# Sliding-window attention and a gated MLP in one kernel: first batch rearranged, work taken off GpSimd, and a new planned order

## The chip, the cores and the metric

One core of a Trainium2 chip. The metric is the time of one execution on the device in microseconds (us), median of several runs. Engines: TensorE (PE; PEld is its weight load), VectorE (DVE), ScalarE (ACT), GpSimd (POOL) and SyncE (SP). DMAs are issued here by GpSimd (loads that also turn float32 into bfloat16) and by SyncE (stores, transposing DMAs).

## The reference

```
q, k, v: [8 batches, 8 heads, 576, 64]
scores = q k^T / 8
heads 0-3: keep 0 <= row - col < 32                            (plain)
heads 4-7: keep 0 <= row - col < 128, (row - col) % 4 == 0     (dilated)
x = softmax(masked scores) v, heads side by side               # [4608, 512]
h = x w_in                                                     # w_in [512, 2048]
g = h / (1 + exp(-beta h))                                     # beta [2048]
out = g w_out                                                  # w_out [2048, 512], float32
```

## The kernel before

The MLP (called the MoE part in the code) runs over 9 tiles of 512 tokens. For each tile, `slot_h` makes 16 blocks of 128 columns of h (line 901: four matmuls of 512 columns over the four parts of x, `xT`), a tanh on ScalarE (line 910) and the gate on VectorE (line 915, into `g`). `block` makes 4 blocks of 128 output rows (line 936: 16 matmuls each, in four parts of four), an eviction (line 951 or 953) and a store (line 956). x for a tile comes from `attention(b)`, which works out batch b, so batch 0 must be done before the first matmul of line 901, and the other batches are worked out between the matmuls of earlier tiles.

`attention` for batches 0 to 2 (`DIRECT = 3`) loads q and k to `st`, transposes them on TensorE (lines 483 and 493) and evicts them to `dk`, `dq`, `kT`, `qT`; later batches go by a bfloat16 copy in DRAM (`s`) and transposing DMAs. Names: S2, S3 are dilated scores (line 697), S00 to S11 plain scores (line 761; line 725 from batch 3 on), T the tail's; V and U are values (lines 802, 818, 787), each followed by a reciprocal and a multiplication on VectorE (lines 652, 653); X and Y carry x back by transposes (lines 855, 870, 840) and copies into `xT`, in batches 0 and 1; later batches use DMAs. In `exp_and_mask` the exp is on ScalarE (line 633). Batch 0 adds its masks on TensorE, with `add_d` and `add_p`, before the scores; later batches multiply by `mask_n` or `mask_d` afterwards (line 637), on GpSimd or VectorE. `spread` copies the values from where they landed (`vd16`) to `vd`, where each row of 64 has a 1 behind it, so that the value matmul also gives the sum. `halo` copies the last 32 rows of each block of `vp` to the next block. Copies all go through line 257, loads through line 408.

Nothing is issued in program order. Each step is a `plan.op` with the engines that could do it, their costs in ns, its dependences and a due time `vt`. `Plan.run` is a list scheduler: it takes the step that can start first, among nearly equal ones that with the earliest due time, and writes each engine's instructions in the order found. `NUDGE` shifts the start that it sees for single steps, `CAPS` says how many PSUM banks each kind of step may hold ("o" are output blocks), and `DVE` and `POOL` exclude each other for steps marked `sbuf`. Where TensorE would be idle for long, the planner puts in fillers, matmuls of zeros (line 1057: twelve small ones, for the first nine; line 1059: one of 256 columns). At run time only semaphores set the times, and each engine follows its written order.

The weights are loaded once: `w_in_bf` in three DMAs (512, 512 and 1024 columns), `w_out_bf` in two halves, all on GpSimd's queue among the loads of batches 0 and 1. The first four h blocks are split (`APART = 4`): first the dilated half of x, then the plain half in two pieces of tokens.

Of the kernel before, what the change touches and what calls it, by code (L numbers as in the profile page):

```python
# [10 lines left out]
ACT = mybir.ActivationFunctionType  # L11
# [3 lines left out]
COLD = 5500  # L15
# [25 lines left out]
class Plan:  # L41
# [4 lines left out]
    CAPS = {"h": 4, "p": 4, "o": 3, "z": 4, "a": 8, "s": 5, "w": 6}  # L46
    SWITCH = 95
    NUDGE = {6: 2500, 32: -2500, 44: 150, 45: -400, 58: -150, 72: 60, 76: -400, 88: -400, 96: 60,
# [10 lines left out]
    LAT = {"PE": 210, "ACT": 45, "DVE": 45, "POOL": 60, "SP": 0}  # L59
    NEAR = {"PE": 40, "ACT": 60, "DVE": 60, "POOL": 60, "SP": 0}  # L60
# [12 lines left out]
    def run(self, filler=None, filler_until=0.0):  # L73
# [14 lines left out]
        halves = False  # L88
        issued = 0.0
        port = {"DVE": 0.0, "POOL": 0.0}  # L90
# [20 lines left out]
        while n_left:  # L111
            best = None
            near = {}
            for o in avail:
# [3 lines left out]
                if o.sbuf and "POOL" in at:  # L118
                    at["POOL"] = max(at["POOL"], issued)
                if o.sbuf:  # L120
                    at = {e: max(t, port["DVE" if e == "POOL" else "POOL"]) for e, t in at.items()}
# [19 lines left out]
            if filler is not None and s <= filler_until and free["PE"] + (300 if free["PE"] < COLD else 170) < s:  # L141
# [5 lines left out]
                free["PE"] = now + (225 if now < COLD else 115)  # L147
# [12 lines left out]
            free[e] = s + d  # L160
            if o.sbuf:
                port[e] = s + d
            elif o.dma and e == "POOL":
                issued = s + d + 1200
# [34 lines left out]
def kernel(  # L199
# [39 lines left out]
    AT_ONCE = 3  # L239

# [91 lines left out]
    fill1 = plan.op([("DVE", 300)], t_fill1, vt=-8)  # L332
# [4 lines left out]
    fill2 = plan.op([("DVE", 1500)], t_fill2, vt=-7.9)  # L337
# [13 lines left out]
    fill4 = plan.op([("POOL", 800)], t_fill4, vt=-1.2)  # L351
# [35 lines left out]
    adds = {"D": plan.op([("POOL", 900)], t_add_d, vt=-8.96)}  # L387
    adds["P"] = plan.op([("POOL", 1250)], t_add_p, vt=-7.5)
    par = plan.op([("DVE", 600)], t_parity, [ident], vt=-7.9)
    mask_tail = plan.op([("POOL", 1150)], t_mask_t, [par], vt=-7.295)  # L390
# [30 lines left out]
    def first_keys():  # L421
# [5 lines left out]
        return [plan.op([("ACT", 175 + .834 * RD * D), ("DVE", 160 + 1.042 * RD * D)],  # L427
                        lambda e, x=x: copy(e, std[0][:, x], stage[:, x]), [o], -9.1, sbuf=True) for x in range(2)]

    def direct_vp(b, deps, vt):  # L430
# [3 lines left out]
        for hs in ((slice(0, 4),) if b else (slice(0, 2), slice(2, 4))):  # L434
# [7 lines left out]
            out.append(plan.op([("DVE", 160 + .27 * n * 320), ("POOL", 170 + 1.04 * n * 320)], halo, [o],  # L442
# [108 lines left out]
    def attention(b, ld, names, vts):  # L551
# [43 lines left out]
        o = plan.op([("DVE", 450), ("POOL", 550), ("ACT", 500)], mixed,  # L595
# [5 lines left out]
        for c in range(2):  # L601
# [4 lines left out]
            o = plan.op([("DVE", 250), ("POOL", 500), ("ACT", 290)], padded,  # L606
# [12 lines left out]
        def spread(e):  # L619
            copy(e, vd[kv][:, :, :, 0:D], vd16_of[b])  # L620
        o = plan.op([("POOL", 1100), ("DVE", 620), ("ACT", 1030)], spread,
                    [ld["vd"][0], (fill3, fill4)[kv]] + war(("vd", kv)), vt, sbuf=True)
        used("vd16" if b < DIRECT else ("st", kv), o)
        wrote(("vd", kv))
        vdeps["D"] = [o]
# [4 lines left out]
        def exp_and_mask(key, sop, g, vt, n, sc, w, m, tiles):  # L630
# [3 lines left out]
            ex = plan.op([act(n)], expo, [sop, fill2] + war(*tiles), vt - .005, group=g)  # L634
            if b >= ADDED or key == ("T",):
                def mask(e):
                    E[e].tensor_tensor(out=w(), in0=w(), in1=m(), op=ALU.mult)  # L637
                ex = plan.op([("POOL", 170 + 2.2 * n), ("DVE", 160 + .8 * n)], mask,
                             [ex] + [mask_tail if key == ("T",) else mask_ops["D" if key[0] in (2, 3) else "n"]],
                             vt, sbuf=True)  # L640
# [3 lines left out]
        def normed(key, vop, g, vt, n, blocks, pv, dst, war_key):  # L644
# [11 lines left out]
            vdone[key] = plan.op([("DVE", 310 + 1.042 * blocks * D)], norm, [vop] + war(war_key), vt - .003, group=g)  # L656

        for name in [n for n in names if n[0] in "ST"]:
# [54 lines left out]
            j = int(name[2])  # L713
            if b >= AT_ONCE:
# [56 lines left out]
            for n, x in enumerate(xs):  # L771
                for h in range(2):
# [5 lines left out]
                                 [("pt", x, i) for i in range(3 * j, 3 * j + 3)])  # L778
        for name in [n for n in names if n[0] in "VU"]:
# [17 lines left out]
            if x >= 2:  # L797
                def values(e, x=x, j=j, g=g):
                    pv = bank(g)[:, 0:4 * (D + 1)].rearrange("p (r h e) -> p r h e", r=2, h=2)
                    for r in range(2):  # L800
                        for a in range(2):
                            nc.tensor.matmul(pv[:, r, a], lhsT=ptd[:, x - 2, j, 2 * r + a],  # L802
                                             rhs=vd[kv][:, 2 * (x - 2) + a, 2 * r + j, 0:D + 1],
                                             start=True, stop=True)
                vop = plan.op([("PE", 4 * mm(D + 1))], values, [sdone[x, j]] + vdeps["D"], vt, acquire=g)
# [287 lines left out]
```

## Time and profile before

| what | us |
|---|---|
| median of 3 runs (299.75 to 299.88) | 299.83 |
| profiled execution: span from first to last instruction | 298.3 |
| the profiled execution's own time | not given apart from its span |
| TensorE busy | 293.0 (98%) |
| VectorE busy | 186.1 (62%) |
| ScalarE busy | 169.8 (57%) |
| GpSimd busy | 90.4 (30%) |
| first matmul of line 901 starts at | 18.44 |
| last store issued at | 295.59 |

The page shows busy times and the chain of waits that ended last. A window row gives the busy time of each engine in a stretch. A timeline row gives start, length, engine, line, operation, what is written and read, and the idle time in front with what ended it. A DMA row gives size and the median time from issue to landing. A group row gives busy time and mean ns of one instruction, then the idle time in front. Matmuls are pipelined, so that the lengths of neighbours overlap.

### The profile page before, as it was taken

How to read it: one execution, taken by the hardware profiler on the slowest of the kernel's cores; microseconds unless marked ns; L12 is line 12 of the kernel's file. 1: busy time of each engine (PE TensorE's matmuls, PEld its weight loads, DVE VectorE, ACT ScalarE, POOL GpSimd, SP SyncE). 2: the span in 40 equal slices, each digit the busy share in tenths (PEclk: the TensorE clock that was granted, in tenths of full speed). 3: DMA queues.
4: the chain of work that ended last, by engine and by line, in shares of the span. 5: the costliest groups of instructions: out<-in, count | busy, mean ns of one | idle time of the engine just before them, and what ended most of it. 6: DMA issues, size and time to landing. Idle time of an engine off the chain costs nothing.

```text
span 298.3 us, 6224 instructions
## 1 busy us (share of the span) xinstructions
PE 293.0 (98%) x2424; PEld 149.8 (50%) x2424; DVE 186.1 (62%) x422; ACT 169.8 (57%) x308; POOL 90.4 (30%) x126
## 2 busy tenths in 40 slices
PE   8999999999999999999999999999999999999995
PEld 6765456545554445444544454445444444444454
DVE  4879668888767658774589358936891075433300
ACT  3768876867456738642487348634862376445311
POOL 8987354654283026600551065000100000000000
PEclk9999999999999999999999999999999999999999
DMA  7999999999979995999999989995115200010122
GB/s 150 187 208 202 206 196 210 154 163 184 185 124 226 151 199 124 171 136 240 184 188 155 200 174 196 162 186 147 38 31 124 73 0 36 35 37 37 63 76 73
DMA packets 111249, 42.00 MB, mean 141 GB/s; under 512 B 87620, under 2 KB 104596, under 8 KB 111220
## 3 DMA queue, kind: packets, MB, share of 16 engines
q0 software_dynamic: 60336, 18.58, 59.6%
q1 hardware_dynamic: 50740, 22.95, 36.4%
q8 instruction: 19, 0.31, 0.4%
q10 hardware_dynamic: 144, 0.07, 0.1%
q14 instruction: 10, 0.08, 0.1%
HBM read 37.76 MB, written 18.87 MB: 190 GB/s over the span
## 4 chain that ended last, share of the span: by engine, by line
PE 86%; DMA 8%; POOL 2%; DVE 1%; issue 1%; ACT 0%; POOLq 0%
PE bank L936 42%; PE bank L901 36%; DMA w_out_bf<-in_moe_w_out_dram 6%; DMA w_in_bf<-in_moe_w_in_dram 2%; PE bank L818 2%; PE bank L697 1%; PE bank L802 1%; PE bank L725 1%; POOL vp L408 1%; PE bank L787 1%; PE bank L666 0%; PE bank L761 0%; POOL st L408 0%; DVE g L915 0%; PE bank L493 0%
## 5 line engine op out<-in xcount | busy, mean ns | idle before, releaser
L936 PE MATMUL bank<-w_out_bf,g 128*128 128x512 bf16 (+2 forms) x608 | 136.6, 368 | 0.4 <-DMA w_out_bf<-in_moe_w_out_dram 0.4
L901 PE MATMUL bank<-xT,w_in_bf 128*128 128x512 bf16 (+2 forms) x584 | 134.8, 376 | 0.1
L915 DVE SCALAR_TENSOR_TENSOR g<-tnh,bank 128x512 bf16<-128x512 bf16 x144 | 96.5, 683 | 51.5 <-ACT tnh L910 50.3
L910 ACT ACTIVATE tnh<-bank,beta_half 128x512 bf16<-128x512 f32 x144 | 98.4, 690 | 53.2 <-PE bank L901 47.4
L901 PEld LDWEIGHTS <-w_in_bf 128*128 128x128 bf16 x584 | 55.1, 98 | 60.6 <-issue 0.2
L936 PEld LDWEIGHTS <-g 128*128 128x128 bf16 x608 | 55.2, 98 | 57.8 <-DMA w_out_bf<-in_moe_w_out_dram 0.5
L951 ACT ACTIVATE osb<-bank 128x512 f32<-128x512 f32 (+1 forms) x30 | 17.6, 592 | 34.1 <-PE bank L936 29.5
L633 ACT ACTIVATE ptd<-bank 128x512 bf16<-128x512 f32 x32 | 17.0, 600 | 21.4 <-PE bank L697 21.4
L633 ACT ACTIVATE pt<-bank 128x384 bf16<-128x384 f32 (+1 forms) x54 | 21.1, 463 | 6.5 <-PE bank L725 4.1
L637 DVE TENSOR_TENSOR pt<-pt,mask_n 128x384 bf16<-128x384 bf16 (+1 forms) x39 | 14.5, 378 | 12.1 <-ACT pt L633 11.6
L653 DVE TENSOR_TENSOR xsp<-bank,rcp 96x384 bf16<-96x384 f32 x32 | 17.7, 554 | 1.1
L637 DVE TENSOR_TENSOR ptd<-ptd,mask_d 128x512 bf16<-128x512 bf16 x25 | 10.9, 448 | 11.3 <-ACT ptd L633 10.4
L953 DVE TENSOR_SCALAR osb<-bank 128x512 f32<-128x512 f32 (+2 forms) x8 | 4.9, 607 | 20.5 <-PE bank L936 20.5
L652 DVE RECIPROCAL rcp<-bank 128x4 f32<-128x4 f32 (+2 forms) x72 | 12.8, 177 | 3.5 <-PE bank L818 1.4
L408 POOL DMA_DIRECT2D vt<-in_v_dram x16 | 13.7, 864 | 4.0 <-DMA w_out_bf<-in_moe_w_out_dram 2.9
L637 POOL TENSOR_TENSOR pt<-pt,mask_n 128x288 bf16<-128x288 bf16 (+1 forms) x7 | 5.3, 764 | 31.2 <-ACT pt L633 31.2
L653 DVE TENSOR_TENSOR xdm<-bank,rcp 128x256 bf16<-128x256 f32 x32 | 13.6, 424 | 1.1
L408 POOL DMA_DIRECT2D s<-in_k_dram x10 | 12.9, 1286 | 0.6 <-issue 0.6
L1015 POOL COPY pace<-xT 1x2 bf16<-1x2 bf16 x4 | 0.7, 176 | 39.2 <-DMA xT<-x 39.2
L408 POOL DMA_DIRECT2D s<-in_q_dram x10 | 12.2, 1220 | 0.1
L818 PEld LDWEIGHTS <-pt 128*128 128x128 bf16 x192 | 8.9, 97 | 4.4
L408 POOL DMA_DIRECT2D vp<-in_v_dram x9 | 10.2, 1129 | 1.0 <-DVE g L915 0.8
(113 smaller groups left out, 186.8 us busy)
## 6 DMA issues: line engine op xcount, KB each, us to landing
out_dram<-osb SPq DMA_DIRECT2D x35, 256.0 KB, 3.8
s<-in_q_dram POOLq DMA_DIRECT2D x10, 288.0 KB, 10.2
s<-in_k_dram POOLq DMA_DIRECT2D x10, 288.0 KB, 9.0
w_out_bf<-in_moe_w_out_dram POOLq DMA_DIRECT2D x2, 1024.0 KB, 17.4
vp<-in_v_dram POOLq DMA_DIRECT2D x7, 288.0 KB, 13.5
st<-in_q_dram POOLq DMA_DIRECT2D x6, 288.0 KB, 10.0
x<-xsp SPq DMA_DIRECT2D x12, 144.0 KB
st<-in_k_dram POOLq DMA_DIRECT2D x5, 288.0 KB, 13.2
```

Source lines behind the costliest of these rows:

```text
L408: {"POOL": nc.gpsimd, "SP": nc.sync}[queue].dma_start(out=out, in_=in_)
L633: nc.scalar.activation(out=w(), in_=sc(), func=ACT.Exp, scale=SCALE)
L637: E[e].tensor_tensor(out=w(), in0=w(), in1=m(), op=ALU.mult)
L652: nc.vector.reciprocal(out=r, in_=p[..., D])
L653: nc.vector.tensor_tensor(out=dst, in0=p[..., 0:D], in1=r.unsqueeze(len(p.shape) - 1).to_broadcast(list(p.shape[:-1]) + [D]), op=ALU.mult)
L818: nc.tensor.matmul(pv[:, a, h2, :], lhsT=lhs, rhs=vp[kv][:, (2 * x + h2) * NI + 3 * j + a, 0:D + 1], start=True, stop=True)
L901: nc.tensor.matmul(bank(g)[:, a:z], lhsT=w_in_bf[:, kt, fb * P:(fb + 1) * P], rhs=xT[:, kt, xo + a:xo + z], start=(i == 0 and kt == kts[0] ...
L910: nc.scalar.activation(out=th[:, 0:n], in_=bank(g)[:, 0:n], func=ACT.Tanh, scale=beta_half[:, fb:fb + 1])
L915: nc.vector.scalar_tensor_tensor(out=g_t[t % 2][:, fb, c0:c0 + n], in0=th[:, 0:n], scalar=1.0, in1=bank(g)[:, 0:n], op0=ALU.add, op1=ALU.mult)
L936: nc.tensor.matmul(bank(g)[:, lo:hi], lhsT=g_t[t % 2][:, fb, tb * P:(tb + 1) * P], rhs=w_out_bf[:, fb, lo:hi], start=(fb == 0), stop=(fb = ...
L951: nc.scalar.mul(out=ob[:, lo:hi], in_=bank(g)[:, lo:hi], mul=0.5)
L953: nc.vector.tensor_single_scalar(out=ob[:, lo:hi], in_=bank(g)[:, lo:hi], scalar=0.5, op=ALU.mult)
```

## The change

Batch 0: plain scores come in three pairs of four blocks (384 columns) in place of four pairs of three (288), and their tiles lie as in the later batches (`FOURS`). Dilated values are read from `vd16` directly, and a one-column matmul with a column of ones gives the sum, so `spread` isn't done (`LANDED`). The copy of the dilated x back to `xT` is one per part rather than two (`WHOLE`). For all batches: masks are multiplied on VectorE only; the copies `mixed`, `padded`, `spread` and `halo` on VectorE or ScalarE, not GpSimd. `w_in` comes in five loads, `w_out` in four, the first two quarters due before batch 1's loads and the last two after its values. The last store is issued by SyncE. The planner's costs are changed, its rule for VectorE and GpSimd is by intervals, the first fillers are counted instead of timed, "o" may hold four banks, and `NUDGE` has 808 entries instead of 85.

```diff
-COLD = 5500
+COLD = 9
-    CAPS = {"h": 4, "p": 4, "o": 3, "z": 4, "a": 8, "s": 5, "w": 6}
+    CAPS = {"h": 4, "p": 4, "o": 4, "z": 4, "a": 8, "s": 5, "w": 6}
-    NUDGE = {6: 2500, 32: -2500, 44: 150,
...
+    NUDGE = {4: 60, 5: -60, 10: 900, 11: 150,
...
+    OVER = {"PE": 0, "ACT": 115, "DVE": 80, "POOL": 0, "SP": 0}
...
-            if filler is not None and s <= filler_until and free["PE"] + (300 if free["PE"] < COLD else 170) < s:
+            if filler is not None and s <= filler_until and free["PE"] + (330 if n_fill < COLD else 170) < s:
...
-                free["PE"] = now + (225 if now < COLD else 115)
+                free["PE"] = now + (316 if n_fill <= COLD else 112)
...
-            free[e] = s + d
+            free[e] = s + d - self.OVER[e]
...
+    LANDED = 1
+    WHOLE = 1
+    FOURS = 1
...
-            out.append(plan.op([("DVE", 160 + .27 * n * 320), ("POOL", 170 + 1.04 * n * 320)], halo, [o],
+            out.append(plan.op([("DVE", 200 + .23 * n * 320), ("ACT", 175 + .834 * n * 320)], halo, [o],
...
-        o = plan.op([("DVE", 450), ("POOL", 550), ("ACT", 500)], mixed,
+        o = plan.op([("DVE", 380), ("ACT", 500)], mixed,
...
-            o = plan.op([("DVE", 250), ("POOL", 500), ("ACT", 290)], padded,
+            o = plan.op([("DVE", 220), ("ACT", 290)], padded,
...
-        o = plan.op([("POOL", 1100), ("DVE", 620), ("ACT", 1030)], spread,
...
+        if b >= LANDED:
+            o = plan.op([("DVE", 430), ("ACT", 1030)], spread,
...
+        else:
+            vdeps["D"] = [ld["vd"][0], fill3]
...
-                ex = plan.op([("POOL", 170 + 2.2 * n), ("DVE", 160 + .8 * n)], mask,
+                ex = plan.op([("DVE", 105 + .62 * n)], mask,
...
+            if b < FOURS:
+                if x and j:
+                    continue
+                m = 2 * j + x
+                blocks = range(4 * m, 4 * m + 4)
...
+                for h in range(2):
+                    exp_and_mask(("P", 2 * m + h), sop, gs[h], vt, 4 * QT,
...
+                            src, n = (vd[kv], D + 1) if b >= LANDED else (vd16, D)
+                            nc.tensor.matmul(pv[:, r, a, 0:n], lhsT=ptd[:, x - 2, j, 2 * r + a],
+                                             rhs=src[:, 2 * (x - 2) + a, 2 * r + j, 0:n],
                                              start=True, stop=True)
...
+                            if b < LANDED:
+                                nc.tensor.matmul(pv[:, r, a, D:D + 1], lhsT=ptd[:, x - 2, j, 2 * r + a],
+                                                 rhs=vd[0][:, 0, 0, D:D + 1], start=True, stop=True)
...
-                for j, (t0, t1) in enumerate(((0, CT // 2), (CT // 2, P))):
+                for j, (t0, t1) in enumerate(((0, P),) if b < WHOLE else ((0, CT // 2), (CT // 2, P))):
...
-        so = plan.op([("ACT" if last_one and hi == HD else "SP", 400)],
-                     lambda e: (nc.scalar if e == "ACT" else nc.sync).dma_start(out=out[r0:r0 + P, lo:hi], in_=ob[:, lo:hi]),
+        so = plan.op([("SP", 400)],
+                     lambda e: nc.sync.dma_start(out=out[r0:r0 + P, lo:hi], in_=ob[:, lo:hi]),
...
-    for n, (c0, c1) in enumerate(((0, 512), (512, 1024), (1024, 2048))):
+    for n, (c0, c1) in enumerate(((0, 256), (256, 512), (512, 1024), (1024, 1536), (1536, 2048))):
...
+                           [], (-7.257, -7.256, -7.182, -7.181)[n], 1024, .41)
```

More of the change, by code (lines that the diff above doesn't have):

```diff
@@ L89, in run @@
         issued = 0.0
-        port = {"DVE": 0.0, "POOL": 0.0}
+        shared = []
+        n_fill = 0
         def release(now):
@@ L117, in run @@
                              if o.group is not None and e != "PE" else [free[e], base]) for e, d in o.engs}
[L118 removed]
+                if o.sbuf == 1 and "POOL" in at:
                     at["POOL"] = max(at["POOL"], issued)
                 if o.sbuf:
[L121 removed]
+                    for e in at:
+                        t = at[e]
+                        for x, a, z, whole in shared:
+                            if a <= t < z and (x, e) in (("POOL", "DVE"), ("DVE", "POOL")) and (whole or o.sbuf == 1):
+                                at[e] = max(at[e], z)
                 fin = min(at[e] + d for e, d in o.engs)
@@ L159, in run @@
                 d += self.SWITCH
-            free[e] = s + d
[L161 to L164, printed above, removed]
+            free[e] = s + d - self.OVER[e]
+            if e in ("DVE", "POOL") and (o.sbuf or o.dma):
+                shared = [x for x in shared if x[2] > s - 3000] + [(e, s, s + d, bool(o.sbuf))]
+                if o.dma:
+                    issued = s + d + 1200
             o.start, o.end = s, s + d + self.LAT[e]
```

96 lines of the change are left out of this document (64 added, 32 removed), and 104 rows, old and new, of the table NUDGE.

## The prediction

> **What bounds the kernel now.** I read the page first, then the busy time by windows.
>
> ```profile
> span 298.3 us, 6224 instructions
> ...
> PE 86%; DMA 8%; POOL 2%; DVE 1%; issue 1%; ACT 0%; POOLq 0%
> ```
>
> ```profile
> 12.00:18.44 6.44, 6.11 (x134) 4.77 (x131) 5.90 (x21) 4.08 (x13) 5.42 (x9) 1.00 1.36 199
> 18.44:52.09 33.65, 33.26 (x373) 18.24 (x364) 24.80 (x59) 25.91 (x53) 19.41 (x29) 1.00 1.39 204
> 18.44:295.20 276.76, 276.23 (x2040) 136.50 (x2030) 172.68 (x377) 159.22 (x285) 74.64 (x93) 1.00 0.96 139
> 295.20:298.30 3.10, 0.00 (x0) 0.00 (x0) 0.29 (x1) 0.11 (x1) 0.00 (x0) 0.87 0.27 84
> ```
>
> The columns of a window are its length, then busy time of PE, PEld, DVE, ACT, POOL, then granted clock, DMA share and GB/s. TensorE owns 86% of the chain of waits, the last line of the first fence. From 18.44, the first matmul of the MoE part, to 295.20 it lacks only 276.76 - 276.23 = 0.5 us of being always busy. So the kernel is three pieces: a start of 18.44 us, a stream of 276.76 us that is bound by TensorE, and a tail of 3.10 us. The median of the runs, 299.83, is 1.53 above the span; no separate time is given for the profiled execution, so I take 1.53 as what lies around its span and its own time as equal to the median.
>
> In the start TensorE is not the limit. This is the timeline of batch 0 there, and the filler matmuls of line 1059 (multiplications by zero):
>
> ```profile
> 9.00:18.44 9.44, 3.19 (x21) 1.51 (x19) 1.00 1.49 192
> ```
>
> ```profile
> 12.03 0.43 DVE L257 COPY vd<-vd 128x1024 bf16<-128x1024 bf16 x1
> 12.57 0.41 PE L802 MATMUL bank<-vd,ptd 128*128 128x65 bf16 x8
> 12.69 0.42 DVE L257 COPY vp<-vp 32x640 bf16<-32x640 bf16 x1 [0.23 <-DMA vp<-in_v_dram]
> 14.23 0.32 DVE L257 COPY vp<-vp 32x640 bf16<-32x640 bf16 x1
> 15.72 0.40 ACT L257 COPY xT<-bank 128x288 bf16<-128x288 bf16 x1
> 17.02 0.76 DVE L257 COPY xT<-bank 128x288 bf16<-128x288 bf16 x2
> 18.03 0.48 PE L493 MATMUL bank<-ident_b,st 64*64 64x64 bf16 x36 [0.25 <-DMA st<-in_q_dram]
> 18.44 1.04 PE L901 MATMUL bank<-xT,w_in_bf 128*128 128x512 bf16 x4
> ```
>
> From 9.00 to 18.44 fillers take 3.19 us of TensorE, while from 12.00 on VectorE is busy 5.90 of 6.44 us. So VectorE (divisions, copies) bounds the last third of the start. The dilated half of x is in xT at 17.02 + 0.76 = 17.78; the stream begins 0.66 later, since transposes of batch 1 stand in front and wait 0.25 for their load. The plain half follows while the first four slots, split by halves, run on the dilated one.
>
> The second limit is the load queue of GpSimd. Issues (start, length), then issue to landing:
>
> ```profile
> 6.32 1.76 POOL L408 DMA_DIRECT2D vp<-in_v_dram  x2
> 9.58 0.78 POOL L408 DMA_DIRECT2D w_in_bf<-in_moe_w_in_dram  x1
> 11.49 0.72 POOL L408 DMA_DIRECT2D st<-in_q_dram  x1
> 12.20 1.51 POOL L408 DMA_DIRECT2D w_in_bf<-in_moe_w_in_dram  x2
> 16.78 0.91 POOL L408 DMA_DIRECT2D w_out_bf<-in_moe_w_out_dram  x1 [0.44 <-DMA w_in_bf<-in_moe_w_in_dram]
> 25.71 0.90 POOL L408 DMA_DIRECT2D w_out_bf<-in_moe_w_out_dram  x1 [0.66 <-DMA w_in_bf<-in_moe_w_in_dram]
> ```
>
> ```profile
> vp<-in_v_dram POOLq DMA_DIRECT2D x2, 144.0 KB, 6.4
> w_in_bf<-in_moe_w_in_dram POOLq DMA_DIRECT2D x1, 512.0 KB, 6.9
> w_in_bf<-in_moe_w_in_dram POOLq DMA_DIRECT2D x1, 512.0 KB, 8.3
> w_in_bf<-in_moe_w_in_dram POOLq DMA_DIRECT2D x1, 1024.0 KB, 12.5
> w_out_bf<-in_moe_w_out_dram POOLq DMA_DIRECT2D x1, 1024.0 KB, 18.0
> w_out_bf<-in_moe_w_out_dram POOLq DMA_DIRECT2D x1, 1024.0 KB, 16.7
> ```
>
> Issue plus landing: batch 0's second vp 7.2 + 6.4 = 13.6; w_in 16.5, 20.5 and 12.95 + 12.5 = 25.4; w_out 34.8 and 42.4, with batch 1's vp still to come. The loads land one behind the other: 1 MB in 25.4 - 20.5 = 4.9 us. Whatever their order, batch 0, the weights and batch 1 are not all there before about 43. The 0.39 us that TensorE lacks between 18.44 and 52.09 is the wait for w_out's first half at 34.8: the stream is just fed, and a stream that starts earlier meets the loads earlier.
>
> **The change, part by part, with its costs.**
>
> ```profile
> L633 ACT ACTIVATE pt<-bank 128x384 bf16<-128x384 f32 x30 | 12.6, 501 | 4.1 <-PE bank L725 4.1
> L633 ACT ACTIVATE pt<-bank 128x288 bf16<-128x288 f32 x24 | 8.5, 415 | 2.4 <-PE bank L761 2.2
> ```
>
> Values used where landed (LANDED): batch 0's copy at 12.03 goes, 0.43 us of VectorE on the path, since the values behind it start at 12.57. Added are 16 one-column matmuls. No row shows one; below nothing is excluded, as they only add work, and the 65-column rows, eight in 0.41 us, bound each at about 0.05, 0.8 in all. I take 0.4, the middle, beside 3.19 us of fillers: nothing; without that cover it costs 0.4.
>
> Wider plain scores (FOURS): 6 exps of 384 in place of 8 of 288, 8 x 0.415 - 6 x 0.501 = 0.31 us less ScalarE. A value step now waits for four exps instead of two; by the longer exps that is up to 1.0 us for the first one, while the dilated divisions keep VectorE busy: nothing, with 1.0 as its upper end.
>
> Whole copies (WHOLE): the four x copies of the dilated half (two on ScalarE, the first 0.40, and two on VectorE, 0.76: some 1.5 on two engines) become two of 512 columns, at ScalarE's 0.60 or so (576 columns would be twice 288 at 0.40, less one start): 0.3 less.
>
> Copies off GpSimd: in batch 0 the vp copies (0.42 + 0.32) may now go to ScalarE, which has 6.44 - 4.08 = 2.4 us free. From 12.00 on, VectorE and ScalarE together then carry 5.90 + 4.08 - 0.43 - 0.31 - 0.3 = 8.9, or 4.5 each if evenly shared, against 5.90 on VectorE now. The gain of the start lies between 0.4 (only the spread is gained) and 1.9 (6.44 - 4.5); dependent steps won't share evenly, so I take three quarters of the upper end: **1.4 us**, the stream at 17.0.
>
> Weights in finer pieces: w_in in five and w_out in four, with two w_out quarters asked for ahead of batch 1 and two behind its values. If the queue has that order, counting on from 13.6 at 4.9 us per MB: w_in 14.9, 16.1, 18.6, 21.0, 23.5; w_out quarters 25.9, 28.4; batch 0's tail and batch 1, 1.84 MB, to 37.4; w_out's third quarter 39.8. Counted back from the end, all is there at 42.4 + 1.4 for batch 1's vp = 43.8, and the third quarter one quarter (2.5) before: 41.3. I take the later one. Hence no piece of w_in holds a start at 17.0, and w_out's first half is there when 16 slots are done. This removes the 0.39 us wait. Next late would be that third quarter. Four more issues on GpSimd take about 0.8 us each; its mask building waits behind them, and nothing on TensorE needs the masks before batch 1's exps, after 28.
>
> ```profile
> 96.49 8.63 PE bank L901 x40
> ```
>
> A matmul of 512 columns takes 8.63 / 40 = 0.216 us. From 17.0, 64 in W_in and 32 in the first half of W_out last until 17.0 + 20.7 = 37.7; attention work in between adds up to 33.26 - 128 x 0.216 = 5.6 us. So the queue of work reaches to between 37.7 and 43.3, and needs to reach 41.3. Batch 1's transposes and scores are ready by then, so I cost this at nothing; its other end is 41.3 - 37.7 = 3.6 us.
>
> Batch 1's transposes (0.41 us from 18.03 to 18.44) move into the stream: +0.41, as their load now lands later.
>
> Masks and copies off GpSimd in batches 1 to 7: more VectorE work, priced in the rivals; at nothing here, as TensorE waits 0.5 us in 276.
>
> The last store: SyncE instead of ScalarE.
>
> ```profile
> 295.34 0.33 SPq L956 DMA_DIRECT2D out_dram<-osb  x1
> 295.59 0.37 ACTq L956 DMA_DIRECT2D out_dram<-osb  x1
> DMA to landing us min/median/max: 1.6/2.0/8.5
> ```
>
> SyncE is free at 295.67, so its issue ends at 296.00 instead of 295.96: +0.04. Landing at the median, 2.0, instead of 1.6 would make it +0.44.
>
> The new order (NUDGE, a fourth output bank, the costs in the planner) sets the rest of the stream anew: no row prices it. With 0.5 us idle there it can win 0.5 in waits and some tenths in switches, and lose as much; I take 0.
>
> Sum: 18.44 - 1.4 + 276.76 + 0.41 - 0.39 + 3.10 + 0.04 = 296.96, plus 1.53: **298.5 us**, 1.3 less than now.
>
> **The rivals.**
>
> The lead is given back at the weights. If little attention work is ready, TensorE waits for w_out's third quarter; at about the lead, 1.3 of the 3.6 us, that gives 299.8. For it speaks the saturated queue; against it, that batch 1's transposes, scores and their divisions need no weights.
>
> A larger lead. The stream starts at 16.5 (the whole 1.9 us) and the transposes of batch 1 stay within the fillers: 298.5 - 0.5 - 0.41 = 297.6. w_in's second piece, 16.1, allows no more than another 0.4.
>
> Slower: VectorE becomes the bound in batches 1 and 2.
>
> ```profile
> 60.00:80.00 20.00, 20.00 (x175) 10.08 (x174) 16.35 (x41) 13.00 (x28) 9.17 (x11) 1.00 1.55 176
> ...
> 60.00:80.00 20.00, 4.04 (x11) 3.30 (x4) 1.00 1.55 176
> ...
> 60.00:80.00 20.00, 0.00 (x0) 0.29 (x1) 4.10 (x4) 1.00 1.55 176
> ```
>
> Between 60 and 80 VectorE is busy 16.35 of 20 us, and GpSimd has four masks (3.30 us, second row, line 637) and four copies (4.10, third row, line 257). On VectorE a mask takes 4.04 / 11 = 0.37 and a copy like the one at 12.03 0.43, so it would carry 16.35 + 4 x 0.37 + 4 x 0.43 = 19.6 of 20. If the gates of line 915 then come late, g and the banks come late, and TensorE waits. Hidden it costs nothing; wholly exposed 3.2, that is 298.5 + 3.2 = 301.7. It decides from 1.3 us exposed. Against it: ScalarE, 13.0 of 20, can take the copies.
>
> Each further piece of a load costs something fixed. From 16.5 to 20.5 two transfers (288 KB for the row at 11.49 and 512 KB) landed in 4.0 us, against 3.8 by the 4.9 per MB of a single one: at most 0.1 each, 0.4 for four. Were it 2 us, w_out's third quarter would come up to 6 us later (three pieces more ahead of it), 47.3 against work to 43.3 at best: a stall of 4.0, 302.5. The Trainium skill, "DMA: Bandwidth & Descriptors", section on the anatomy of one DMA on the GpSimd path, gives about 2.0 us fixed per transfer, and its measured bandwidths ask for transfers of 1 MB or more, which speaks against this split; here, with many in flight, the trace does not agree.
>
> **How the numbers follow.** The forecast, 298.5: 0.56. Larger lead, 297.6: 0.15. Lead given back, 299.8: 0.17, of which 0.05 keeps more than 0.2%. VectorE as bound, 301.7: 0.10; the pieces, 302.5: 0.02. Faster by over 0.2% (0.6 us, about what a measurement here can tell from no change): 0.56 + 0.15 + 0.05 = 0.76; within it 0.12; slower 0.12. The range 297.2 to 299.9 leaves out the slower cases and the far ends of the bounds.
>
> **What would show it.** The first row of line 901 at 17.0, not after 18; no copy to vd in batch 0 and six plain exps; w_in's first piece landing by 15; no wait for w_out near 34.8; TensorE idle under 1 us after the stream's start; a tail of about 3.1. The prediction is wrong if line 901 still begins after 18, if TensorE waits near 38 to 41 for w_out, or if VectorE's window from 60 to 80 rises above 19 with waits of TensorE in it.

## The result and the profile after

The changed kernel takes 302.59 us (median; four runs, 302.12 to 303.93) against 299.79 for the kernel before on the same chip: a ratio of 1.0102, 95% interval 1.0078 to 1.0126. It is 2.8 us slower, where 1.3 us faster was forecast. The profiled execution took 302.12 us, 2.29 above that of before. The profiled execution of before is taken as 299.83, the first of its runs. All experiments are told as ratios to the kernel before, measured beside them, since its median moved between 299.79 and 300.43 from one group of runs to the next. One execution, of d_q, was over 1.5% above the fastest of its kernel at a granted clock of 0.992 and is left out of its ratio.

The lines of the changed kernel are numbered anew: the w_in matmul is line 1047 (901 before), the w_out matmul 1082 (936), the evictions 1097 and 1099 (951, 953), the store 1102 (956), the long filler 1204 (1059), masks 734 (637), divisions 749 and 750 (652, 653), copies 351 (257), loads 502 (408), the transposing DMAs that bring q and k from `s` 568 (474), those that bring x to `xT` 641 (547). In the runs of the experiments the lines are shifted by what each edit puts in ahead of them.

The page, and the busy time by windows (columns as in the prediction):

```profile
span 300.4 us, 6142 instructions
...
PE 80%; DMA 11%; POOL 3%; SPq 2%; issue 2%; DVE 1%; POOLq 0%; DVEq 0%
```

```profile
12.00:17.64 5.64, 5.39 (x111) 4.09 (x106) 4.55 (x15) 5.31 (x12) 4.11 (x10) 1.00 1.55 195
...
60.00:80.00 20.00, 19.79 (x181) 10.10 (x184) 17.84 (x47) 15.79 (x32) 2.16 (x2) 1.00 1.58 174
```

TensorE's share of the chain fell from 86 to 80%, waits on transfers grew from 8 to 11%, and SyncE's queue came in with 2%. Some matmul records are missing in this trace, so I compare by the weight loads (PEld), which are complete in both. This is the stream's start by weight loads, first before, then after:

```profile
18.03 0.36 PEld L493 LDWEIGHTS <-st 64*64 64x64 bf16 x36 [0.37 <-DMA st<-in_q_dram]
18.44 0.55 PEld L901 LDWEIGHTS <-w_in_bf 128*128 128x128 bf16 x4
```

```profile
17.64 0.12 PEld L1047 LDWEIGHTS <-w_in_bf 128*128 128x128 bf16 x2
...
18.77 0.16 PEld L1016 LDWEIGHTS <-xsp 96*128 96x128 bf16 x3 [0.44 <-DVE xsp L750]
...
19.13 0.37 PEld L763 LDWEIGHTS <-dkt 128*128 128x128 bf16 x4
...
19.82 0.10 PEld L1204 LDWEIGHTS <-zero 128*128 128x128 bf16 x1
...
21.39 0.10 PEld L1204 LDWEIGHTS <-zero 128*128 128x128 bf16 x1
21.51 1.02 PEld L1047 LDWEIGHTS <-w_in_bf 128*128 128x128 bf16 x8
23.07 0.98 PEld L1047 LDWEIGHTS <-w_in_bf 128*128 128x128 bf16 x6 [0.54 <-DMA w_in_bf<-in_moe_w_in_dram]
...
33.17 0.31 PEld L1204 LDWEIGHTS <-zero 128*128 128x128 bf16 x2
```

The stream starts at 17.64 instead of 18.44, but batch 0 isn't through by then: the transposes of its plain x (xsp) and the tail's scores (dkt) follow, one waits on a division, and four fillers stand inside the stream. At 23.07 TensorE waits for a piece of w_in: the written order has the ninth block of the first tile (fb = 8) ahead of blocks 5 to 7, so its piece is wanted one piece early.

The second place is SyncE's queue, before and after:

```profile
98.70 6.76 SPq L547 DMA_TRANSPOSE xT<-x  x2
```

```profile
96.22 1.85 SPq L641 DMA_TRANSPOSE xT<-x  x1
98.12 4.42 SPq L568 DMA_TRANSPOSE dq<-s  x1
102.64 2.69 SPq L641 DMA_TRANSPOSE xT<-x  x1
```

```profile
107.13 2.47 PEld L1082 LDWEIGHTS <-g 128*128 128x128 bf16 x12
110.36 2.29 PEld L1047 LDWEIGHTS <-w_in_bf 128*128 128x128 bf16 x12 [0.76 <-issue]
```

A transpose for batch 4 (98.12) stands between the two that bring batch 3's x; the second landed at 110.26 and TensorE waited until 110.36. (The trace has six pairs of transposes into xT, for batches 2 to 7, and this is the second; the expectations below call the batches 2 and 3 where they are 3 and 4.) "issue" in that row only means that this view names no releaser; the view of waits lists it as xT.

The third is the end. Before, two stores on two queues closed it (the rows at 295.34 and 295.59 in the prediction). After:

```profile
295.59 1.04 ACT L1097 ACTIVATE osb<-bank 128x512 f32<-128x512 f32 x2 [1.62 <-PE bank L1082]
```

```profile
296.53 0.29 DVE L1099 TENSOR_SCALAR osb<-bank 128x128 f32<-128x128 f32 x1 [8.43 <-PE bank L1082]
```

```profile
293.99 3.69 SPq L1102 DMA_DIRECT2D out_dram<-osb  x4
```

The last full block now ends together with the narrow cuts, both of ScalarE's last evictions come one behind the other, and three stores queue on SyncE until 293.99 + 3.69 = 297.68; before the last one was issued by 295.96.

The account of the two profiled executions, in us:

| part | before | after | difference |
|---|---|---|---|
| start, to the first w_in weight load | 18.44 | 17.64 | -0.80 |
| stream, to the last w_out weight load | 276.46 | 278.52 | +2.06 |
| tail, to the end of the span | 3.35 | 4.25 | +0.90 |
| around the span (298.25 and 300.41 unrounded) | 1.58 | 1.71 | +0.13 |

Within the stream I find +0.94 for the four fillers and what they cover, +0.43 for the w_in piece, +0.90 at three places for the x that comes back by SyncE (0.64, 0.13, 0.13), +0.32 for xsp, and some +0.7 of work that stood ahead of the stream before (36 transposes of q 0.41, twelve weight loads of the tail's scores and of xsp); against them -0.4 to -0.6 for the w_out wait, which is gone. That is 2.7 to 2.9; the stream also changes to small matmuls and back 66 times instead of 72, by the weight loads, which I take for the other side of the account, though no run tests it. These are prices from one execution each, and they vary: in c_tail below, whose order is the same there, the gap at 110.99 was 1.34 us where it is 0.76 here. The split between start and stream varies more: in the runs below that keep the order up to there, the first w_in weight load came at 17.31 to 18.37 by the changed order and at 18.44 to 19.01 by the old one.

### The profile page after: what moved, and what is told of

It reads as the page before. It is cut to its first block, busy times and chain, and to the rows that moved or that the text cites. A ratio compares the mean times of both kernels' runs of the same rounds, so it can differ in the third digit from the quotient of the medians.

```text
span 300.4 us, 6142 instructions
## 1 busy us (share of the span) xinstructions
PE 291.7 (97%) x2398; PEld 150.1 (50%) x2437; DVE 184.3 (61%) x426; ACT 177.6 (59%) x322; POOL 73.2 (24%) x107
## 4 chain that ended last, share of the span: by engine, by line
PE 80%; DMA 11%; POOL 3%; SPq 2%; issue 2%; DVE 1%; POOLq 0%; DVEq 0%
PE bank L1082 38%; PE bank L1047 34%; DMA w_in_bf<-in_moe_w_in_dram 4%; DMA x<-xsp 3%; DMA xT<-x 3%; DMA x<-xdm 2%; SPq L568 1%; PE bank L964 1%; PE bank L794 1%; PE bank L942 1%; PE bank L863 1%; PE bank L577 1%; POOL w_in_bf L502 1%; PE bank L926 1%; SPq L641 1%
## 5 line engine op out<-in xcount | busy, mean ns | idle before, releaser
L1082 PE MATMUL bank<-w_out_bf,g 128*128 128x512 bf16 (+2 forms) x586 | 134.3, 367 | 1.8 <-issue 1.0
L1047 PE MATMUL bank<-xT,w_in_bf 128*128 128x512 bf16 (+1 forms) x567 | 133.6, 376 | 1.1 <-DMA xT<-x 0.3
L1056 ACT ACTIVATE tnh<-bank,beta_half 128x512 bf16<-128x512 f32 x144 | 96.1, 687 | 57.8 <-PE bank L1047 47.8
L1097 ACT ACTIVATE osb<-bank 128x512 f32<-128x512 f32 (+2 forms) x33 | 19.2, 580 | 33.1 <-PE bank L1082 30.2
L749 DVE RECIPROCAL rcp<-bank 96x6 f32<-96x6 f32 (+2 forms) x72 | 12.9, 179 | 5.5 <-PE bank L964 2.5
L502 POOL DMA_DIRECT2D s<-in_q_dram x10 | 13.7, 1366 | 0.5 <-issue 0.5
L502 POOL DMA_DIRECT2D vt<-in_v_dram x16 | 12.6, 794 | 2.4 <-DMA w_in_bf<-in_moe_w_in_dram 1.5
L502 POOL DMA_DIRECT2D s<-in_k_dram x10 | 11.1, 1108 | 0.5 <-issue 0.3
L1099 DVE TENSOR_SCALAR osb<-bank 128x512 f32<-128x512 f32 (+1 forms) x5 | 3.0, 609 | 12.9 <-PE bank L1082 12.9
L964 PE MATMUL bank<-vp,pt 128*128 128x65 bf16 x192 | 9.1, 193 | 0.0
```

The lines of the kernel that those rows point to most:

```text
L502: {"POOL": nc.gpsimd, "SP": nc.sync}[queue].dma_start(out=out, in_=in_)
L749: nc.vector.reciprocal(out=r, in_=p[..., D])
L964: nc.tensor.matmul(pv[:, a, h2, :], lhsT=lhs, rhs=vp[kv][:, (2 * x + h2) * NI + 3 * j + a, 0:D + 1], start=True, stop=True)
L1047: nc.tensor.matmul(bank(g)[:, a:z], lhsT=w_in_bf[:, kt, fb * P:(fb + 1) * P], rhs=xT[:, kt, xo + a:xo + z], start=(i == 0 and kt == kts[0] ...
L1056: nc.scalar.activation(out=th[:, 0:n], in_=bank(g)[:, 0:n], func=ACT.Tanh, scale=beta_half[:, fb:fb + 1])
L1082: nc.tensor.matmul(bank(g)[:, lo:hi], lhsT=g_t[t % 2][:, fb, tb * P:(tb + 1) * P], rhs=w_out_bf[:, fb, lo:hi], start=(fb == 0), stop=(fb = ...
```

## The experiments

All edits act between planning and issuing: `todo` is the planner's list of steps with their engines, numbered as created; nothing is planned anew, so the rest of the order stays. My theory after the traces: the loss sits in the new order, at the named places. The rivals: one of the parts does it (masks and copies off GpSimd, the weight pieces, the last store), or the loss is spread. The wider plain scores (`FOURS`), the fourth output bank and `NUDGE` have no run of their own.

**Mending the changed kernel's order.** Four runs together; two of the edits are told in words.

a_tail:

```diff
+ the last full block (steps 1275 to 1278) ahead of the cuts, brought forward
+ evictions in turn by VectorE and ScalarE
```

> The changed kernel with its own order, except at the end: the last full block of 512 columns is finished before the three cuts of the last block, and the two smaller evictions alternate between VectorE and ScalarE, as in the kernel before; all stores stay on SyncE. Order theory: the changed kernel's tail, 4.25 us from the last weight load to the end of the span, falls to about 3.4, and the time by 0.7 to 0.9, to 301.7 to 301.9. Queue theory (the single SyncE queue itself costs the time): the tail stays above 3.9 and the time above 302.2. Engine theory (work moved to VectorE and ScalarE slows the stream): no matter for the tail, the stream stays at 278.5.

a_xt:

```diff
+ todo.insert(at(659), todo.pop(at(582)))   # batch 3's second xT ahead of batch 4's transpose
```

> The changed kernel with one move: on SyncE the second transposing DMA of batch 2's x (into xT) goes ahead of a transposing DMA of batch 3 that waits for its copy in DRAM. Order theory: the wait of TensorE near 109.5 us (0.64 us, with 0.13 at 114.4) goes, the time falls by 0.5 to 0.8 to about 301.9, and the runs scatter less than the changed kernel's 302.1 to 303.9. Engine theory: the wait has another cause, so it stays and the time moves by less than 0.3.

a_slot:

```diff
+ block fb = 8 of tile 0 takes the place and bank of fb = 7, blocks 5 to 7 move up
+ fillers behind the first w_in matmul dropped
```

> The changed kernel with block 8 of the first tile put behind blocks 5 to 7, each in the others' places and banks, and without the four fillers that stand inside the stream. Order theory: the wait for w_in of 0.43 us at 22.4 goes; the fillers (0.9 us from their load to the next) stand partly where TensorE waits anyway, so 0.4 to 1.0 us in all, 301.6 to 302.2. Load theory (the loads themselves are late and bound this stretch): the wait moves to the next block and the time stays within 0.2 of 302.6.

a_all has all three:

> The three edits together. Order theory: they are at separate places, so they add up: 1.6 to 2.7 us less, 299.9 to 301.0, and scatter below 0.5. Engine theory: at most 1.2 of it (the tail and a little), 301.4 or more, the rest coming back as waits at the next places.

Measured (the changed kernel itself: 1.0102): a_tail 1.0114 (1.0061 to 1.0168), a_xt 1.0064 (1.0041 to 1.0087), a_slot 1.0078 (1.0046 to 1.0109), a_all 1.0063 (1.0039 to 1.0087). The single intervals overlap that of the changed kernel; all point estimates but a_tail's are lower. The three edits didn't add up: a_all's 301.94 is above the 299.9 to 301.0 that separate places would give. In a_xt the second transpose runs right behind the first and the wait is gone, though the last w_out weight load came no earlier (296.20 against 296.16). The answering rows:

```profile
96.48 6.35 SPq L655 DMA_TRANSPOSE xT<-x  x2
```

```profile
107.63 2.47 PEld L1096 LDWEIGHTS <-g 128*128 128x128 bf16 x12
110.22 2.47 PEld L1061 LDWEIGHTS <-w_in_bf 128*128 128x128 bf16 x12
```

a_tail shortened the tail from 4.25 to 3.76 and paid for it in a new place. I had brought the block ahead of the eviction that frees its bank:

```profile
288.10 1.61 PEld L1100 LDWEIGHTS <-g 128*128 128x128 bf16 x8
290.72 1.28 PEld L1100 LDWEIGHTS <-g 128*128 128x128 bf16 x8 [1.01 <-issue]
```

**The parts alone, on the order before.** Here the order before is kept as it is and one part of the change is done in it.

b_off: every step of the kind `halo`, `mixed`, `padded`, `spread`, `mask` on POOL gets DVE in its place (23 steps).

> The kernel before, its written order kept, with every mask multiply and every halo, mixed, padded and spread copy that GpSimd ran issued by VectorE at the same place of the order. Order theory (the changed kernel lost its time to the new order: the work put behind the start of the stream, its waits and its tail): this edit alone stays within 0.5 us of 299.8, VectorE has room for it in the stages where TensorE is the bound. Engine theory (taking the steps off GpSimd loads VectorE until it holds TensorE): over 1.0 us slower, with waits of TensorE on VectorE in the batches' stages. In batch 0, before 18.4 us, the four spread copies move from GpSimd onto VectorE too, which by the engine theory moves the first w_in matmul later than 18.4.

(One detail in it is wrong: the four spread copies on GpSimd belong to batches 3, 4, 6 and 7, not to batch 0.)

b_st: `todo[at(1301)][1] = "SP"`.

> The kernel before, its order kept, with the last store issued by SyncE instead of ScalarE. The span from the last w_out weight load to the end was 3.35 us before and 4.25 after. If the store's queue alone made this, the time rises by 0.5 to 0.9 us; if the order of the last evictions did (the order theory), it stays within 0.3 us of 299.8, since the two stores before it are 0.25 us apart and would then be issued some 0.3 to 0.6 us apart on one queue.

b_land: LANDED and WHOLE for batch 0, and the copies that they make needless are dropped.

> The kernel before, its order kept, with batch 0's values read where the transfer put them (four spread copies dropped, a one-column matmul for each sum of weights) and its first normalized tiles copied whole. Start theory (as the prediction had it: the chain in front of the first w_in matmul shortens by the copies): the first w_in matmul comes 0.3 to 1.0 us earlier than 18.44 and the time falls by as much, to 298.8 to 299.5. Moved-work theory (what the changed kernel gained at its start was work put behind it): the first w_in matmul within 0.3 us of 18.44, time within 0.3 of 299.8.

b_w:

```diff
+ cuts = ((0, 256, 512), (512, 1024), (1024, 1536, 2048))[n]   # w_in, one dma for each piece
+ ... for a in (2 * n, 2 * n + 1)                              # w_out, quarters
```

> The kernel before, its order kept, with w_in in five transfers and w_out in four at the places of the queue where three and two stood, the same bytes. Bytes theory (a transfer queued behind another costs its bytes, at about 4.9 us for 1 MB in fp32): the last quarter of w_out lands within 0.5 us of 42.44, its first quarter some 5 us ahead of 34.77 and the wait of TensorE for w_out near 34.4 (0.39 us) is gone: 299.4 to 299.9. Piece theory (a fixed 2 us for each transfer): the last quarter lands 8 us later than 42.44 and TensorE waits for it, 300.5 or more.

Measured: b_off 1.0061 (1.0039 to 1.0083), b_st 1.0008 (0.9998 to 1.0019), b_land 0.9995 (0.9986 to 1.0005), b_w 1.0006 (0.9992 to 1.0020). So the store, the values where landed and the pieces cost nothing that can be told, and bring nothing either. Only b_off is slower, by 1.8 us, as the engine theory said. (The traced execution of b_w is its slowest, 302.40 with a median of 300.39.) b_land's expectation of an earlier first w_in matmul failed: 36 transposes of batch 1's q stand in front of it and wait for their transfer (the row at 18.03 above, 18.93 here); the shorter chain ahead of them is of no use. The first w_in weight load came even 0.89 later than in the trace of before, and yet the last weight load of w_out ended at 295.07, against 295.00. Before (its start is shown above), then b_land:

```profile
289.97 5.03 PEld L936 LDWEIGHTS <-g 128*128 128x128 bf16 x52
```

```profile
19.33 0.55 PEld L920 LDWEIGHTS <-w_in_bf 128*128 128x128 bf16 x4
...
290.04 5.03 PEld L955 LDWEIGHTS <-g 128*128 128x128 bf16 x52
```

So what the start loses or gains isn't what the end shows. In the trace of before the lead was spent in the wait for w_out near 34.8; in b_land, b_mask and b_off, which start at 18.80 to 19.33, that wait isn't there.

So b_off was taken apart, the copies now with the engines that the changed kernel gives them; the same steps were given back to GpSimd in the changed kernel; and the transposes of b_land's finding were moved.

b_mask: ten masks to VectorE.

> The kernel before, its order kept, with only the ten mask multiplies that GpSimd ran given to VectorE at the same place (GpSimd 740 to 1150 ns each, VectorE 300 to 450). With all 23 steps on VectorE the time rose by 1.6 to 1.8 us. Mask theory (a mask that joins VectorE's queue in its place holds what stands behind it until its exponential is there): 0.8 us or more slower than before. Copy theory (the 13 copies of transposed and landed tiles make the loss): within 0.4 us of before.

b_copy: thirteen copies to VectorE or ScalarE.

> The kernel before, its order kept, with only the 13 halo, mixed, padded and spread copies taken off GpSimd, each to the engine (VectorE or ScalarE) that the changed kernel gives it. Copy theory: 0.8 us or more slower than before, with waits of TensorE on VectorE or ScalarE where batches 2 to 4 are prepared (48 to 120 us). Mask theory: within 0.4 us of before.

c_pool: the changed kernel, the same 23 steps on POOL.

> The changed kernel, its order kept, with the same ten masks and 13 copies given back to GpSimd at the places where the changed kernel has them on VectorE and ScalarE. Engine theory (leaving GpSimd costs some 1.7 us in the changed kernel too): 301.0 or less. Order theory (the changed kernel's order was made for the faster engines, its loss is elsewhere): 302.3 or more, since each mask now takes 0.4 to 0.7 us longer ahead of the values that wait for it.

b_move:

```diff
+ a, b = todo.pop(at(215)), todo.pop(at(218))   # q transposes of batch 1, one eviction
+ todo[at(121) + 1:at(121) + 1] = [a, b]        # behind the first eight w_in matmuls
```

> The kernel before, its order kept, with batch 1's 36 q transposes (0.41 us, their transfer landed at 17.99 us) put behind the first eight w_in matmuls instead of ahead of them. Moved-work theory: the first w_in matmul comes 0.4 us or more earlier than without the move, the last w_out matmul at the same time: 299.8 to 300.1, as before. Start theory (an earlier start of the stream is an earlier end): 299.3 to 299.6.

Measured: b_mask 1.0016 (1.0002 to 1.0030), b_copy 1.0041 (1.0025 to 1.0057), c_pool 1.0126 (1.0105 to 1.0146), b_move 1.0010 (0.9998 to 1.0022).

b_copy costs 1.2 us, and its trace shows one place where most of it goes. ScalarE before, then ScalarE, VectorE and TensorE's weight loads of b_copy:

```profile
114.38 0.70 ACT L910 ACTIVATE tnh<-bank,beta_half 128x512 bf16<-128x512 f32 x1
```

```profile
114.27 1.25 ACT L271 COPY vp<-vp 32x1280 bf16<-32x1280 bf16 x1
115.43 0.58 ACT L647 ACTIVATE ptd<-bank 128x512 bf16<-128x512 f32 x1
116.04 0.69 ACT L924 ACTIVATE tnh<-bank,beta_half 128x512 bf16<-128x512 f32 x1
```

```profile
116.76 0.69 DVE L929 SCALAR_TENSOR_TENSOR g<-tnh,bank 128x512 bf16<-128x512 bf16 x1 [1.08 <-ACT tnh L924]
```

```profile
116.35 0.10 PEld L816 LDWEIGHTS <-ptd 128*128 128x128 bf16 x1
117.50 0.16 PEld L816 LDWEIGHTS <-ptd 128*128 128x128 bf16 x3 [1.05 <-issue]
```

A halo copy of 1.25 us takes the place of the tanh, which comes 1.66 us later than in the trace of before; the gate follows it, the bank that the gate reads comes free late, and the values of batch 4 stop behind it. I find nothing of the sort in the changed kernel, where the planner put the copies elsewhere. And given back to GpSimd there, the steps make it no faster: 303.46 us, where the engine theory needed 301.0 or less. So in an order that isn't made for it, leaving GpSimd is a loss; that it is none in the changed kernel is likely, but c_pool alone doesn't show it, since that order isn't made for GpSimd either.

b_move tests the start from the other side. The first w_in weight load came at 17.87, 0.57 earlier than before, and the last w_out one at 295.01, against 294.90:

```profile
17.87 0.56 PEld L915 LDWEIGHTS <-w_in_bf 128*128 128x128 bf16 x4
19.11 0.37 PEld L507 LDWEIGHTS <-st 64*64 64x64 bf16 x36 [0.68 <-DMA st<-in_q_dram]
```

The start of the stream moved, the end didn't come earlier: the transposes were done later, and the matmuls behind them waited 0.5 for the eviction.

**What is left.** The end was mended without the new wait, then all four places together, then batch 1's loads.

c_tail: from step 1275, where the changed kernel has it, the full block first, then the 256 columns, then the two cuts; step 1285 to DVE, store 1298 to ACT.

> The changed kernel with the end as in the kernel before: from where the last full block of w_out starts, it runs through all its 16 matmuls, then the 256 columns and the two cuts of 128; evictions by ScalarE, VectorE, ScalarE, VectorE, the last store by ScalarE. Nothing is moved ahead of the eviction that frees its bank. Tail theory (0.9 us of the loss is the stores that queue at the end): the span from the last w_out weight load to the end is 3.3 to 3.4 us instead of 4.25, and the time falls by 0.7 to 0.9, to 301.7 to 301.9. Rival (what the end gives back is paid at another wait): 302.4 or more.

c_fix: a_xt, a_slot and c_tail in one.

> The changed kernel with all four places of its order mended: block 8 of the first tile behind 5 to 7, no fillers inside the stream, batch 2's second transposing transfer ahead of batch 3's crossbar, and the end as in the kernel before. Order theory (the loss is the sum of these places): 0.65 us from the first three (302.59 to 301.94 when the end was ordered otherwise, with a wait of 0.90 us that this end doesn't have) and 0.9 from the end, 300.0 to 301.0. If it stays above 301.5, the loss is spread over the stream and not at these places.

d_all, which is c_fix with this besides:

```diff
+ front = [193, 20, 21, 194]            # batch 1's k, two of v, q
+ todo[at(31):at(31)] = [todo.pop(at(n)) for n in front]   # ahead of w_out's first quarter
```

> The changed kernel with the four places of its order mended as in the run before (302.14 us), and batch 1's first four transfers (k, two of v, q) put ahead of the two w_out quarters in GpSimd's queue, where they stood in the kernel before. Queue theory (the rest of the loss is the weights that were put ahead of batch 1's loads: its k landed at 32.0 us instead of 26.84): the waits of TensorE on k, q and v between 32 and 42 us (0.6, 0.35, 0.3 us beyond the same phases of the changed kernel) go, the stretch from the first w_in to the last w_out weight load falls from 278.5 to 277.3 or less, time 300.9 to 301.2. If the time stays above 301.8, the rest isn't at these landings.

d_q has this edit alone, without the fillers:

> The changed kernel with only the same four transfers put ahead of the two w_out quarters, and without the four fillers inside the stream, which stood where nothing of batch 1 was ready. Queue theory: the fillers (0.94 us) go and no wait takes their place, 301.6 to 301.8. Rival (w_out's second quarter now lands some 4 us later, at about 34.5, and TensorE waits for it, or the four fillers' time turns into another wait, as in the runs without them): 302.3 or more.

Measured: c_tail 1.0069 (1.0052 to 1.0085), c_fix 1.0073 (1.0049 to 1.0097), d_all 1.0044 (1.0027 to 1.0061), d_q 1.0076 (1.0060 to 1.0091; its profiled execution took 306.89 and isn't read). d_q's median, 303.02, lies where its rival had it (302.3 or more): the loads in front and no fillers, without the other mends, bring nothing that can be told. c_tail's tail fell to 3.50 and c_fix's to 3.58, some 0.7 less, as meant, though c_tail's median of 302.22 is above the 301.9 expected, and c_fix stayed at 302.14, above the 301.5 that would have shown the named places to be all. Its waits of TensorE say why, and those of d_all:

```profile
PE bank L978 <- DMA vd<-in_v_dram: 0.5, 1, 0.5
PE bank L613 <- DMA st<-in_k_dram: 0.3, 1, 0.3
PE bank L623 <- DMA st<-in_k_dram: 0.2, 1, 0.2
PE bank L613 <- DMA st<-in_q_dram: 0.2, 1, 0.2
```

```profile
PE bank L1242 <- DVE warm L450: 1.1, 1, 1.1
PE bank L1026 <- DVE xdt L790: 0.2, 1, 0.2
```

Lines 613 and 623 are the transposes of k and q (613 in batch 1; 623, at 55.53, in batch 2), line 978 the dilated values, line 1026 the tail's x. Without the waits in front, the stream reached batch 1's loads before these had landed, because the weights stand ahead of them: k at 32.00 us in c_fix, 26.84 before. Put ahead of w_out in d_all, k lands at 26.64 and all four waits are gone (the first line is of the warm-up, in every kernel); the tail's x now waits 0.2 for a division. The stream falls from 278.49 to 277.85, but 0.39 of that is a later start (18.23 against 17.84): the last w_out weight load comes 0.24 earlier. The ratio's interval (up to 1.0061) lies below that of the changed kernel (from 1.0078); it overlaps c_fix's, so that the loads' own share isn't shown. The expected 277.3 and 301.2 were not reached.

Last, both parts that cost nothing, on the order before: b_land, and w_out's first half in two transfers (e_best).

> The kernel before, its order kept, with batch 0's values read where they landed and its first normalized tiles copied whole (alone: -0.05%), and the first half of w_out in two transfers at the same place of the queue, w_in as it was. With all weights in finer pieces the wait of TensorE for w_out (0.39 us near 34.4) went, and GpSimd's issues of 0.75 us each made other steps later. Bytes theory: only one issue more, which stands where GpSimd waited 0.58 us anyway; the wait for w_out is gone and the time is 0.2 to 0.5 us below the kernel before. Rival (the stream's end doesn't follow: the wait comes back at the next transfer, as it did in the mended kernels): within 0.15 us of before.

Measured: 0.9999 (0.9988 to 1.0010). The wait is gone from the trace and the time is the same, so no version beat the kernel before.

What stays open: of the loss of 1.0%, the five mended places account together for about 0.6 (1.0102 to 1.0044). The rest, 0.44% or 1.3 us, isn't found at one place: d_all still has 0.24 us more tail than before, 0.26 in two waits near 114 and 153 us, and the work of the start in its stream; no run separates these.

## Why the prediction was wrong

**The failed step is the term for the new order, which "sets the rest of the stream anew: no row prices it", with "I take 0"** and a bound of half a microsecond and some tenths to either side. Measured, the stream, where this term stands, is the largest part of the loss: +2.06 where +0.02 was forecast; the tail took +0.90 where +0.04 was. Mending five places of the order takes back about 0.6 of the 1.0%; that the rest is the order's too isn't shown. The bound came from the 0.5 us idle in the stream before; but idle time bounds what an order can win, not what another can lose. The part of the change that had no row was taken as the smallest term, and the range left it out.

**Start, -1.4.** Measured -0.80. The work did move off VectorE as said (no vd copy, six exps, busy 4.55 us from 12.00 on), but to ScalarE, which is now the one that is full: 5.31 of 5.64 us. The sum of the two is 9.86 against the 8.9 I worked out. The loads of this execution also landed 0.5 later (batch 0's second q transfer at 10.85 against 10.34), so some of the missing 0.6 may be that.

**What an earlier start is worth.** The sum took the whole start as gain and charged only +0.41 for moved transposes. By b_move, moving them brings nothing; the changed kernel moved some 0.7 us of work. The lead counted in the sum was partly the same work done later. b_land shows the other half: a shorter chain is no gain where a transfer that isn't there yet holds the start, and a start that is 0.89 later needn't make a later end.

**w_out, -0.39.** The step was right, its price was not: no wait near 34.8, its second quarter landed at 30.46. That the pieces cost nothing was right too, the last quarter landed at 44.95 where 43.8 was worked out, and in b_w, at the places of before, at 42.87 against 42.44. The rival of a fixed price for each piece was wrong: at 2 us each it would have put the last quarter some 8 us later. The 2 us are from the Trainium skill, "DMA: Bandwidth & Descriptors", section on the anatomy of one DMA on the GpSimd path (about 2.0 us fixed for each transfer); with transfers queued behind each other the runs do not agree. What the order of the loads did cost is batch 1's k, behind two quarters of w_out: the prediction followed the third quarter and not that. And with the wait removed, e_best (b_land's edit in it) takes 0.9999 of the time before, within 0.0011: the wait of the one trace wasn't 0.39 us that the median could win.

**VectorE as the bound.** Its window from 60 to 80 rose to 17.84, not 19.6, and ScalarE's from 13.00 to 15.79: the copies went there, as the point against this rival said. In the changed kernel the matmuls of its stream show no wait for VectorE; its weight loads have gaps put down to VectorE that add up to 3.1 us, 0.7 before, the longest 0.44. Matmuls still run in part of such a gap, and no run separates them, so a part of the open rest may be here. The mechanism exists (b_off and b_copy), in b_copy at one place of the order and not as a full engine.

**Tail, +0.04.** The store's engine alone is 1.0008 in b_st, with a tail of 3.53 against 3.35. The rest of the +0.90 goes with which block is last: c_tail puts the order of before back, and ScalarE for the last store, and has 3.50. The +0.90 is of one execution: in a_slot and c_pool, whose end is that of the changed kernel, the tail was 3.92 and 3.94.

## What to carry to other kernels

Where a change reissues the whole order of a stream that is always busy, its unknown leans to one side: here there was half a microsecond of idle time to win, and every queue (weights, loads, stores, banks) could get a new wait. Follow each transfer that is moved back, not only the one moved forward, and count an earlier start as gain only for idle time or fillers that it removes. Mend one such wait and look for the next in line before believing its price.

## What was not expected of the hardware

In b_w one mask multiply of VectorE took 2.59 us; the fastest of its form in that run took 0.30. GpSimd ran three masks meanwhile, and TensorE then waited 1.3 us for a division that came behind it on VectorE:

```profile
40.41 0.31 DVE L650 TENSOR_TENSOR pt<-pt,mask_n 128x288 bf16<-128x288 bf16 x1 [0.94 <-ACT pt L646]
40.93 2.59 DVE L650 TENSOR_TENSOR pt<-pt,mask_n 128x288 bf16<-128x288 bf16 x1 [0.22 <-ACT pt L646]
```

```profile
41.24 2.10 POOL L650 TENSOR_TENSOR pt<-pt,mask_n 128x288 bf16<-128x288 bf16 x3
```

The Trainium skill, "SBUF — State Buffer", section on who interferes with whom, says that a VectorE instruction with two inputs in SBUF contends with a GpSimd instruction that reads SBUF and that the one that comes second waits for the other. The rows agree that one is held up while the other works, but not in which: VectorE's mask is recorded from 40.93, GpSimd's first only from 41.24, and it is VectorE's that outlasted all three. Why isn't shown. In the changed kernel, with no such work on GpSimd, no VectorE instruction is over 0.5 us longer than the fastest of its form; before there were two.

The loads of batch 0 land at times that vary from run to run: its second q transfer, issued at 3.63 to 3.70 in all 19 profiled executions, landed between 10.34 (the kernel before, the earliest) and 11.43 us. A start read from one execution is uncertain by some 0.5 us to either side: the first w_in weight load of the changed order came at 17.31 to 18.37.
